# Pooled attention and a cosine MLP: weight differences in tiles of their own, two output buffers, and a first product copied by ScalarE

## The chip, the cores and the metric

The kernel runs on one core of one Trainium2 chip. The metric is device time in microseconds; the time before is the median of three runs. The profile is one execution of the program, with the span of its instructions in microseconds. In it PE is TensorE's matmuls and PEld its weight loads, DVE is VectorE, ACT is ScalarE, POOL is GpSimd and SP is SyncE; L402 is line 402 of the kernel.

## The reference

```
q, k, v: (8, 8, 576, 64) fp32                     # batch, heads, sequence, head size
k_p, v_p = mean of k, v over groups of 8 positions       # 72 pooled positions
attn = softmax(q @ k_p.T / sqrt(64)) @ v_p
x = attn with the heads side by side                     # 4608 tokens x 512
h = x @ w_in                                             # 512 x 2048
out = (h * cos(h)) @ w_out                               # 2048 x 512, fp32 out
```

## The kernel before

The 4608 tokens are nine tiles of 512, t = 0 to 8, and the eight batches of attention are woven into them: while tile t goes through the two layers, the attention of batch t + 1 is computed for the tiles to come. The schedule is written out by hand: each engine runs its instructions in the order in which the code gives them, and waits stand only where data or buffers ask for them.

A tile has two stages.

- The up stage, `up_mm` and `up_g`: 64 matmuls of 128x512 (L317) fill pairs of PSUM banks with h, two chunks of 128 hidden rows at a time. ScalarE makes cos of a bank as a Sin with a bias (L327), and VectorE multiplies bank and cosine into `g_sb` in bf16 (L331). The multiplication is what sets a bank free again. From tile 2 on, four pairs of banks go round, one of them the two `obanks`.
- The down stage. Tiles 0 and 1 use plain matmuls (`down_mm`, L334): four blocks of 128 tokens with 16 matmuls each, and a copy of each block by VectorE into an output buffer `o_two` (`down_out`, L339), from which SyncE's queue writes 64 rows at a time. Matmuls of attention stand between them; `fill` lists them with the number of down matmuls that stand ahead.

From tile 2 on (`FIRST = 2`) the down stage is a 2x2 block product with seven block products in place of eight (`down_products`). The tokens are halved (256 and 256), the hidden rows are halved (`HF` = 8 chunks of 128), the output columns are halved (`HM` = 256). Each product has 16 matmuls of 128x256 (L402) in one of two accumulators, A and Bb, each a PSUM bank; in the last tile each is two banks (`apart`), so that its halves can be read one by one. The products need sums of g, made by VectorE (`put_g12` L363 and L364, `put_g3` L368, `put_g4` L372, each in two halves: the first half in the up stage, the second in the down stage), and sums of w_out, which are made once. With b11, b12, b21, b22 the blocks of w_out:

```
w3 = b22 - b12     w2 = w3 + b11     w4 = b21 - w2     and     b12 - b11 for product 3
```

`put_weights` makes w3, w2 and w4 for the first half of the rows on GpSimd at the end of tile 0, and for the second half on VectorE between the up stage's g products of tile 1. The last difference, b12 - b11, is written in place over b12 (`put_first_weights`, L355). That can't be before the plain matmuls of tile 1 have read w_out, so the two instructions stand at the end of tile 1's down stage on VectorE, behind its last output copies and ahead of tile 2's first g product.

The order of the down stage from tile 2 on, from the code, with attention left out:

```
            product(0)
            product(1)
            put_g12(1)
            reads[0]()
            put_g3(1)
            reads[1]()
            put_g4(1)
            product(2)
```

`reads[0]` copies product 0 from A into `p1_sb` (L416); product 2 writes the same bank and so waits for this copy, and it also needs g2 from `put_g12`. `reads[1]` adds p1 to product 1 and writes the first output columns (L418); product 3 writes bank Bb and waits for it. In tiles 2 to 6 the scores of the next batch stand between products 0 and 1. In tile 7 only a small rest of them does, with its Exp on ScalarE, and in tile 8 nothing.

The output buffers of all tiles have one tag, `o_two`, of 128 x 2 x 512 fp32, which is 4 KB of each partition, and three of them go round. GpSimd adds up the groups of eight positions of k and v (`pool_add`, L151 to L159) in each tile up to tile 6, and issues the loads of the next batch.

Of the kernel before, what the change touches and what calls it, by code (L numbers as in the profile page):

```python
# [20 lines left out]
def kernel(  # L21
# [48 lines left out]
    HF, HT, HM = FFCH // 2, TILE // 2, d_model // 2  # L70
    g1, g2, g3, g4 = [wpool.tile([128, HF, HT], BF16, name=f"g{i}") for i in range(1, 5)]

    w2, w3, w4 = [[wpool.tile([128, 4, HM], BF16, name=f"w{k}{i}") for i in range(2)] for k in range(2, 5)]

    SpA = -(-Sp // 16) * 16
    kk = [wpool.tile([128, H, SpA], BF16, name=f"kk{i}") for i in range(2)]
# [258 lines left out]
                         rhs=w_out_sb[fc // 4][:, fc % 4, :], start=(fc == 0), stop=(fc == FFCH - 1))  # L335

    def down_out(t, ms, ps):
        o = msb.tile([128, 2, d_model], FP32, name="o_two", tag="o_two", bufs=3)[:, 0]
        nc.vector.tensor_copy(out=o, in_=ps)  # L339
        rows_of = out.rearrange("(b p t) m -> b t p m", b=B, t=ROW)  # L340
        for i, rows in enumerate(half):
            b_, pos = divmod((t * TILE + ms * 128) // 64 + i, ROW)
            nc.sync.dma_start(out=rows_of[b_, ORDER[pos]], in_=o[rows])

    def put_weights(i, eng, k=None):

        vec = eng.tensor_tensor
        (b11, b12), (b21, b22) = [(w[:, :, 0:HM], w[:, :, HM:]) for w in (w_out_sb[i], w_out_sb[i + 2])]
        for n, (w, x, y, op) in enumerate(((w3, b22, b12, SUB), (w2, w3[i], b11, ADD), (w4, b21, w2[i], SUB))):
            if k in (None, n):  # L350
                vec(out=w[i], in0=x, in1=y, op=op)

    def put_first_weights(i):
        w = w_out_sb[i]
        nc.vector.tensor_tensor(out=w[:, :, HM:], in0=w[:, :, HM:], in1=w[:, :, 0:HM], op=SUB)  # L355

    def g_part(f, t, f0, f1):
        return g_sb[:, f * HF + f0:f * HF + f1, t * HT:(t + 1) * HT]
# [15 lines left out]
    def down_products(t):  # L374

        def of(w, m=0):
            return lambda fc: w[fc // 4][:, fc % 4, m * HM:(m + 1) * HM]

        def part(x):
            return lambda fc, p: x[:, fc, p * 128:(p + 1) * 128]  # L380

        apart = t == NT - 1
        if apart:
            A, Bb = [[x[:, 0:HM] for x in two] for two in (obanks, (banks[1][:, 0, :], banks[2][:, 0, :]))]
        else:
            A, Bb = [[obanks[i][:, p * HM:(p + 1) * HM] for p in range(2)] for i in (1, 0)]
        products = [
            (A, True, part(g_part(0, 0, 0, HF)), of(w_out_sb[0:2])),
            (Bb, True, part(g_part(1, 0, 0, HF)), of(w_out_sb[2:4])),
            (A, True, part(g2), of(w2)),  # L390
            (Bb, True, part(g1), of(w_out_sb[0:2], 1)),
            (A, False, part(g3), of(w3)),
            (Bb, False, part(g4), of(w_out_sb[2:4], 1)),
            (A, False, part(g_part(1, 1, 0, HF)), of(w4)),
        ]
        mms = []
        for n, (bank, first, g, w) in enumerate(products):
            order = [(fc, p) for fc in range(HF) for p in range(2)]
            if apart and n == 6:
                order.sort(key=lambda x: x[1])  # L400
            for fc, p in order:
                mms.append(lambda bank=bank, first=first, g=g, w=w, fc=fc, p=p: nc.tensor.matmul(  # L402
                    bank[p], lhsT=g(fc, p), rhs=w(fc),
                    start=(first and fc == 0 and (apart or p == 0)), stop=(fc == HF - 1 and (apart or p == 1)),
                    skip_group_check=not first))

        p1, v16, q15 = [msb.tile([128, 2, HM], FP32, name=n, tag=n, bufs=1) for n in ("p1_sb", "v_sb", "q_sb")]
        o1, o2 = [msb.tile([128, 2, d_model], FP32, name="o_two", tag="o_two", bufs=3) for _ in range(2)]
        m1, m2 = slice(0, HM), slice(HM, d_model)

        def each(out, bank, other=None, m=slice(0, HM), tk=None):

            for p in range(2) if apart else (slice(0, 2),):
                ps = bank[p] if apart else obanks[1 if bank is A else 0].rearrange("p (a m) -> p a m", a=2)
                if other is None:
                    nc.vector.tensor_copy(out=out[:, p, m], in_=ps)  # L416
                else:
                    nc.vector.tensor_tensor(out=out[:, p, m], in0=ps, in1=other[:, p], op=ADD)  # L418
                if apart and tk is not None:
                    rows_out(t, tk, out, (p,), m, (nc.sync, nc.scalar))  # L420

        reads = [
            lambda: each(p1, A),
            lambda: each(o1, Bb, p1, m1, 0),
            lambda: each(v16, A, p1),
            lambda: each(q15, Bb, p1),
            lambda: each(o2, A, q15, m2, 1),
            lambda: (each(o1, Bb, v16, m2, 0), apart or rows_out(t, 0, o1)),
            lambda: (each(o2, A, p1, m1, 1), apart or rows_out(t, 1, o2)),
        ]  # L430
        return [mms[i * 2 * HF:(i + 1) * 2 * HF] for i in range(7)], reads
# [99 lines left out]
    for t in range(NT):  # L531
# [5 lines left out]
        for n, fp in enumerate(up_order(t)):  # L537
            up_mm(t, fp, 2 if n < 2 else 0)
            between = ()
            if t == 0:  # L540
                if fp == 4:
                    puts = pool_k_mm(1, obanks[0], 0, 2), pool_k_mm(1, obanks[1], 2, 4)
                elif fp in (5, 6):
                    g0 = 9 * (fp - 5)
                    puts = q_transpose_mm(1, obanks[0], g0, g0 + 5), q_transpose_mm(1, obanks[1], g0 + 5, g0 + 9)
                if fp in (4, 5, 6):
                    puts[0](vec)
                    between = ((puts[1], act),)
            up_g(t, fp, between)
            if t >= FIRST and 3 <= n < 6:  # L550
                (put_g12, put_g3, put_g4)[n - 3](0)
            if t == 1 and 3 <= n < 6:
                put_weights(1, nc.vector, n - 3)
            if 0 < t and b < B:
                if n == 0:
                    q_transpose(b)
                elif n == 2:
                    k_transpose(b)
# [36 lines left out]
        if t < FIRST:  # L595
            fi = 0
            for n, (ms, fc) in enumerate(mms):
                while fi < len(fill) and fill[fi][0] <= n:
                    fill[fi][1]()
                    fi += 1  # L600
                down_mm(obanks[ms % 2], ms, fc)
                if fc == FFCH - 1:
                    down_out(t, ms, obanks[ms % 2])
            if t + 1 == FIRST:
                for i in range(2):
                    put_first_weights(i)
        else:
            products, reads = down_products(t)

            def product(i, j=0, k=2 * HF):  # L610
                for mm in products[i][j:k]:
                    mm()

            us = BY_TOKENS
            later = []

            u0, u1, u2, u3 = [(b, us[i], banks[j]) for i, j in enumerate((2, 1, 0, 1))]
            ur = (t, REST, banks[2])

            def scores_of(*parts):  # L620
                for part in parts:
                    scores_mm(*part)
                for part in parts:
                    scores_exp(*part)

            def muls():
                while later:
                    later.pop(0)()

            steady, rest = b < B, t < B  # L630
            if rest:
                exp_tables()
            product(0)
            if steady:
                scores_of(u0, u1, u2)
            elif rest:
                scores_of(ur)
# [6 lines that stand above are left out]
            if steady:  # L644
                values(*u0, later)
            product(2)
            reads[2]()
            muls()
            if steady:
                values(*u1, later)  # L650
            product(3)
            reads[3]()
            muls()
            if steady:
                values(*u2, later)
            product(4)
            reads[4]()
            muls()
            if steady:
                scores_of(ur, u3)  # L660
            product(5, 0, 4)
            if rest:
                values(*ur, later)
            product(5, 4, 12)
            muls()
            if steady:
                values(*u3, later)
            product(5, 12)
            reads[5]()
            muls()  # L670
            product(6)
            reads[6]()
# [5 lines left out]
        if b + 1 < B:  # L678
# [1 line left out]
            load_q(b + 1)  # L680
            load_kv(b + 1, "v", v)
            if t == 0:
                put_weights(0, nc.gpsimd)
            pool_add(b + 1, "k")
            pool_add(b + 1, "v")
# [28 lines left out]
```

The softmax here doesn't subtract the row's maximum and nothing guards it: scores larger than these inputs give would overflow.

## Time and profile before

| | us |
|---|---|
| median of three runs (lowest, highest) | 294.95 (294.61, 295.21) |
| span of the profiled execution | 294.5 |
| VectorE: the two in-place differences, L355, start | 86.4 and 88.1 |
| the same, time of each | 1.76 and 1.82 |
| VectorE: copies of product 0, L416, full bank (six) | 0.68 |
| the same, half a bank (two, last tile) | 0.42 |
| TensorE's waits for that copy, in total (three) | 1.6 |
| output transfers, issue to landing: lowest, median, highest | 1.9, 2.4, 5.8 |

A row of a timeline gives start, duration, engine, line, operation, output <- inputs with their shapes, the number of instructions merged, and in brackets the idle time of the engine before it with what ended it. A row of busy times by stretch gives the stretch, its length, and then for each engine the busy time and the number of instructions. In the rows of groups the duration is the mean of one instruction in ns. Idle time of an engine that nobody waits for costs nothing. TensorE's granted clock is 0.999 in this run.

### The profile page before, as it was taken

What the parts mean: (1) busy time and instruction counts of PE and PEld (TensorE: products, weight loads), DVE (VectorE), ACT (ScalarE), POOL (GpSimd) and SP (SyncE); (2) the same over time, 40 slices, a digit from 0 to 9 for tenths busy, and PEclk for the clock granted to TensorE, in tenths of its full rate; (3) what the DMA queues carried; (4) which work ended last, traced back from release to release, by engine and by line L of the source; (5) the groups of instructions that cost most, each with busy time, mean ns of one, the idle gap of its engine ahead of it and who ended that gap; (6) DMA issues with size and microseconds to landing.
All of it is one profiled execution on the core that took longest, in us unless ns stands there. A gap on an engine that the chain in (4) does not pass through costs nothing. (4 is left out here: it accounts for less than half of the span.)

```text
span 294.5 us, 5317 instructions
## 1 busy us (share of the span) xinstructions
PE 282.1 (96%) x2096; PEld 174.0 (59%) x2120; DVE 226.6 (77%) x306; ACT 206.4 (70%) x261; POOL 148.4 (50%) x144
## 2 busy tenths in 40 slices
PE   8899999999999899999999999999999999999984
PEld 3545544444544587458745874588458844774673
DVE  5558547595489998799879887998798879846972
ACT  3786897469767688679967997699769976336500
POOL 8563079993995299536983599349900000000000
PEclk9999999999999999999999999999999999999999
DMA  7999999629817961969185929691840060005014
GB/s 163 205 207 206 207 205 204 139 52 148 168 37 137 139 104 26 200 89 163 19 182 89 169 45 195 92 174 28 173 73 2 4 142 0 2 21 122 2 36 107
DMA packets 44488, 32.95 MB, mean 112 GB/s; under 512 B 22192, under 2 KB 40112, under 8 KB 44464
## 3 DMA queue, kind: packets, MB, share of 16 engines
q0 software_dynamic: 19744, 18.07, 39.2%
q1 hardware_dynamic: 24080, 14.03, 22.2%
q10 hardware_dynamic: 640, 0.52, 0.7%
q8 instruction: 16, 0.26, 0.3%
q14 instruction: 8, 0.07, 0.1%
HBM read 36.70 MB, written 9.44 MB: 157 GB/s over the span
## 5 line engine op out<-in xcount | busy, mean ns | idle before, releaser
L317 PE MATMUL bank<-xT,w_in_sb 128*128 128x512 bf16 x503 | 114.7, 379 | 1.8 <-DVE g_sb L331 0.9
L327 ACT ACTIVATE cos<-bank,half_pi 128x1024 f32<-128x1024 f32 x65 | 71.4, 1113 | 48.5 <-PE bank L317 45.2
L317 PEld LDWEIGHTS <-w_in_sb 128*128 128x128 bf16 x576 | 56.0, 98 | 67.2 <-issue 1.5
L331 DVE TENSOR_TENSOR g_sb<-bank,cos 128x1024 bf16<-128x1024 f32 x65 | 78.4, 1220 | 22.1 <-ACT cos L327 22.0
L151 POOL TENSOR_TENSOR half_sums<-kv_st 72x512 f32<-72x512 bf16 x48 | 56.9, 1212 | 27.3 <-DMA kv_st<-in_k_dram 26.8
L262 DVE TENSOR_TENSOR xT<-bank,inv 64x512 bf16<-64x512 f32 (+1 forms) x72 | 45.3, 629 | 17.9 <-ACT inv L258 16.9
L257 ACT ACTIVATE inv<-bank 64x512 f32<-64x512 f32 (+1 forms) x72 | 39.1, 544 | 12.4 <-PE bank L251 11.2
L402 PEld LDWEIGHTS <-g 128*128 128x128 bf16 x448 | 42.9, 98 | 8.2 <-issue 3.3
L229 ACT ACTIVATE ex<-bank 72x1024 bf16<-72x1024 f32 (+1 forms) x40 | 35.1, 928 | 3.2 <-PE bank L222 3.0
L402 PEld LDWEIGHTS <-g_sb 128*128 128x128 bf16 x336 | 32.1, 98 | 6.9 <-issue 1.0
L153 POOL TENSOR_TENSOR half_sums<-half_sums 72x512 f32<-72x512 f32 x24 | 30.4, 1284 | 0.0
L334 PE MATMUL obank<-w_out_sb,g_sb 128*128 128x512 bf16 x123 | 29.9, 379 | 0.3 <-issue 0.2
L402 PE MATMUL obank<-w,g 128*128 128x256 bf16 x224 | 26.9, 272 | 1.7 <-DVE p_sb L416 1.6
L402 PE MATMUL obank<-w_out_sb,g_sb 128*128 128x256 bf16 x208 | 25.1, 273 | 0.3 <-DVE g_sb L331 0.3
L402 PE MATMUL obank<-w_out_sb,g 128*128 128x256 bf16 x192 | 24.8, 273 | 0.0
L258 ACT ACTIVATE inv<-inv 128x512 f32<-128x512 f32 (+1 forms) x36 | 21.0, 583 | 1.1
L251 PE MATMUL bank<-ex,vz 72*128 72x256 bf16 (+1 forms) x176 | 20.0, 243 | 0.0
L334 PEld LDWEIGHTS <-g_sb 128*128 128x128 bf16 x128 | 11.8, 97 | 12.5 <-issue 1.0
L251 PEld LDWEIGHTS <-vz 72*128 72x128 bf16 x176 | 13.7, 97 | 4.4 <-DVE xT L262 0.5
L156 POOL TENSOR_TENSOR kp<-half_sums 72x512 bf16<-72x512 f32 x12 | 15.0, 1270 | 0.5
L222 PE MATMUL bank<-qT,kk 64*72 64x256 bf16 (+1 forms) x192 | 13.2, 251 | 1.5 <-DVE g_sb L331 0.6
L402 PE MATMUL obank<-w,g_sb 128*128 128x256 bf16 x112 | 13.4, 273 | 0.0
(83 smaller groups left out, 253.6 us busy)
## 6 DMA issues: line engine op xcount, KB each, us to landing
out_dram<-o_two SPq DMA_DIRECT2D x64, 128.0 KB, 2.4
kv_st<-in_v_dram POOLq DMA_DIRECT2D x8, 576.0 KB, 13.6
kv_st<-in_k_dram POOLq DMA_DIRECT2D x7, 576.0 KB, 7.8
q_b<-in_q_dram POOLq DMA_DIRECT2D x6, 576.0 KB, 9.9
w_in_sb<-in_moe_w_in_dram POOLq DMA_DIRECT2D x4, 512.0 KB, 13.1
w_out_sb<-in_moe_w_out_dram POOLq DMA_DIRECT2D x4, 512.0 KB, 18.5
q_b<-in_q_dram POOLq DMA_DIRECT2D x4, 288.0 KB, 11.7
g_sb<-in_k_dram SPq DMA_DIRECT2D x1, 576.0 KB, 3.7
```

The lines of the kernel that those rows point to most:

```text
L151: add(out=s[:, h:h + 2], in0=x[:, h:h + 2, 0:4, :], in1=x[:, h:h + 2, 4:8, :], op=ADD)
L153: add(out=s[:, h:h + 4, 0:2, :], in0=s[:, h:h + 4, 0:2, :], in1=s[:, h:h + 4, 2:4, :], op=ADD)
L229: nc.scalar.activation(out=ex[:, 0:nh * n].rearrange("p (a n) -> p a n", a=2), in_=pair[:Sp, :, 0:nh * n // 2], func=ACTF.Exp, scale=scale ...
L251: nc.tensor.matmul(pair[:, hp, (i // 2) * n:(i // 2 + 1) * n], lhsT=vz[b % 2][:, pj, 2 * hp:2 * hp + 2, :].rearrange("p a d -> p (a d)"), ...
L257: nc.scalar.activation(out=inv[half[1 - hp]], in_=pair[half[1 - hp], hp, 0:w], func=ACTF.Ln)
L258: nc.scalar.activation(out=inv, in_=inv, func=ACTF.Exp, scale=-1.0)
L262: nc.vector.tensor_mul(out=x_out(b, u, half[hp]), in0=cols(pair[half[hp], hp, :], u), in1=cols(inv[half[1 - hp]], u))
L317: nc.tensor.matmul(h[j] if h is obanks else h[:, j, :], lhsT=w_in_sb[fc // 4][:, ki, (fc % 4) * 128:(fc % 4 + 1) * 128], rhs=xT[:, ki, t * ...
L327: nc.scalar.activation(out=c, in_=ps, func=ACTF.Sin, bias=half_pi[:, :1])
L331: nc.vector.tensor_mul(out=o, in0=ps, in1=c)
L334: nc.tensor.matmul(o, lhsT=g_sb[:, fc, ms * 128:(ms + 1) * 128], rhs=w_out_sb[fc // 4][:, fc % 4, :], start=(fc == 0), stop=(fc == FFCH - 1))
L402: mms.append(lambda bank=bank, first=first, g=g, w=w, fc=fc, p=p: nc.tensor.matmul(bank[p], lhsT=g(fc, p), rhs=w(fc), start=(first and fc ...
```

## The change

The differences b12 - b11 get tiles of their own, w1, so that w_out stays as loaded. With that they no longer have to stand behind tile 1's matmuls: they are made on VectorE in tile 1's down stage, one behind its third down matmul and one behind its fifth, in the order of the code. The two tiles take 4 KB of each partition, and one of the three output buffers is given up for them. The third edit moves the copy of product 0 to ScalarE in tiles 7 and 8 (`t >= B - 1`), where VectorE makes the second half of g1 and g2 just ahead of it; the aim is that the bank comes free while VectorE is still at these sums.

```
-    w2, w3, w4 = [[wpool.tile([128, 4, HM], BF16, ...) for i in range(2)] for k in range(2, 5)]
+    w1, w2, w3, w4 = [[wpool.tile([128, 4, HM], BF16, ...) for i in range(2)] for k in range(1, 5)]
...
-        o = msb.tile([128, 2, d_model], FP32, name="o_two", tag="o_two", bufs=3)[:, 0]
+        o = msb.tile([128, 2, d_model], FP32, name="o_two", tag="o_two", bufs=2)[:, 0]
...
-    def put_first_weights(i):
-        w = w_out_sb[i]
-        nc.vector.tensor_tensor(out=w[:, :, HM:], in0=w[:, :, HM:], in1=w[:, :, 0:HM], op=SUB)
+        for k in ks:
+            out, x, y, op = {1: (w1, b12, b11, SUB), 3: (w3, b22, b12, SUB), 2: (w2, w3[i], b11, ADD),
+                             4: (w4, b21, w2[i], SUB)}[k]
+            eng.tensor_tensor(out=out[i], in0=x, in1=y, op=op)
...
-            (Bb, True, part(g1), of(w_out_sb[0:2], 1)),
+            (Bb, True, part(g1), of(w1)),
...
-        o1, o2 = [msb.tile([128, 2, d_model], FP32, name="o_two", tag="o_two", bufs=3) for _ in range(2)]
+        o1, o2 = [msb.tile([128, 2, d_model], FP32, name="o_two", tag="o_two", bufs=2) for _ in range(2)]
...
-                    nc.vector.tensor_copy(out=out[:, p, m], in_=ps)
+                    (nc.scalar.copy if t >= B - 1 else nc.vector.tensor_copy)(out=out[:, p, m], in_=ps)
...
-            if t + 1 == FIRST:
-                for i in range(2):
-                    put_first_weights(i)
+                if t == 1 and n in (2, 4):
+                    put_weights(n // 2 - 1, nc.vector, (1,))
```

The other sums of weights keep their place, their engine and their order.

More of the change, by code (lines that the diff above doesn't have):

```diff
@@ L71 @@
     g1, g2, g3, g4 = [wpool.tile([128, HF, HT], BF16, name=f"g{i}") for i in range(1, 5)]
-    w2, w3, w4 = [[wpool.tile([128, 4, HM], BF16, name=f"w{k}{i}") for i in range(2)] for k in range(2, 5)]
+    w1, w2, w3, w4 = [[wpool.tile([128, 4, HM], BF16, name=f"w{k}{i}") for i in range(2)] for k in range(1, 5)]
     SpA = -(-Sp // 16) * 16
@@ L343, in down_out, with put_weights @@
             nc.sync.dma_start(out=rows_of[b_, ORDER[pos]], in_=o[rows])
-    def put_weights(i, eng, k=None):
-        vec = eng.tensor_tensor
+    def put_weights(i, eng, ks=(1, 3, 2, 4)):
         (b11, b12), (b21, b22) = [(w[:, :, 0:HM], w[:, :, HM:]) for w in (w_out_sb[i], w_out_sb[i + 2])]
-        for n, (w, x, y, op) in enumerate(((w3, b22, b12, SUB), (w2, w3[i], b11, ADD), (w4, b21, w2[i], SUB))):
-            if k in (None, n):
-                vec(out=w[i], in0=x, in1=y, op=op)
-    def put_first_weights(i):
-        w = w_out_sb[i]
-        nc.vector.tensor_tensor(out=w[:, :, HM:], in0=w[:, :, HM:], in1=w[:, :, 0:HM], op=SUB)
+        for k in ks:
+            out, x, y, op = {1: (w1, b12, b11, SUB), 3: (w3, b22, b12, SUB), 2: (w2, w3[i], b11, ADD),
+                             4: (w4, b21, w2[i], SUB)}[k]
+            eng.tensor_tensor(out=out[i], in0=x, in1=y, op=op)
     def g_part(f, t, f0, f1):
@@ L549 @@
             up_g(t, fp, between)
-            if t >= FIRST and 3 <= n < 6:
+            if t == 1 and 3 <= n < 6:
+                put_weights(1, nc.vector, ((3, 2, 4)[n - 3],))
+            if t > 1 and 3 <= n < 6:
                 (put_g12, put_g3, put_g4)[n - 3](0)
-            if t == 1 and 3 <= n < 6:
-                put_weights(1, nc.vector, n - 3)
             if 0 < t and b < B:
@@ L682 @@
             if t == 0:
-                put_weights(0, nc.gpsimd)
+                put_weights(0, nc.gpsimd, (3, 2, 4))
             pool_add(b + 1, "k")
```

## The prediction

> **What bounds the kernel now.** I read the page's busy times first, then busy times cut by tile, then the chain and the waits of TensorE, then the timelines of the tiles that stand out.
>
> ```profile
> PE 282.1 (96%) x2096; PEld 174.0 (59%) x2120; DVE 226.6 (77%) x306; ACT 206.4 (70%) x261; POOL 148.4 (50%) x144
> ```
>
> TensorE is busy 282.1 of 294.5 us, so only what shortens its gaps shortens the kernel. The busy times by stretch, one tile each (tiles 2, 3, 7 and 8, from the first up matmul to the next tile's first), show where the gaps are:
>
> ```profile
> 84.12:116.02 31.90, 30.23 (x223) 19.63 (x224) 30.52 (x37) 23.93 (x31) 23.05 (x21) 1.00 0.58 97
> 116.02:145.95 29.93, 29.67 (x224) 19.68 (x224) 25.93 (x34) 24.10 (x32) 19.18 (x18) 1.00 0.70 121
> ...
> 235.74:263.20 27.46, 26.70 (x193) 17.55 (x193) 21.44 (x28) 14.82 (x17) 0.00 (x0) 1.00 0.17 39
> 263.20:290.57 27.37, 26.42 (x176) 17.11 (x175) 19.95 (x31) 8.96 (x9) 0.00 (x0) 1.00 0.27 60
> ```
>
> The columns are length, then busy time of PE, PEld, DVE, ACT, POOL. Tiles 3 to 6 take 29.93 us each (starts 116.02, 145.95, 175.88, 205.81, 235.74) with one PE wait of 0.16 us. Tile 2 runs the same instructions and takes 1.97 us longer; its DVE is busy 30.52 of 31.90 us. Its timeline tells why:
>
> ```profile
> 86.39 3.49 DVE L355 TENSOR_TENSOR w_out_sb<-w_out_sb 128x1024 bf16<-128x1024 bf16 x2
> ...
> 89.81 3.67 DVE L331 TENSOR_TENSOR g_sb<-bank,cos 128x1024 bf16<-128x1024 f32 x3
> ...
> 97.32 1.89 PE L317 MATMUL bank<-xT,w_in_sb 128*128 128x512 bf16 x8 [0.93 <-DVE g_sb L331]
> ```
>
> The two in-place weight differences stand on DVE ahead of the tile's first g product. That starts at 89.81, 5.7 us after the tile's start; in tile 3 it is 119.96-116.02 = 3.9. TensorE then waits 0.93 us for a bank.
>
> In tiles 7 and 8 the wait is another one, the copy of the first product out of its bank:
>
> ```profile
> 252.88 0.69 DVE L364 TENSOR_TENSOR g<-g,g_sb 128x1024 bf16<-128x1024 bf16 x1
> 253.49 0.68 DVE L416 COPY p_sb<-obank 128x512 f32<-128x512 f32 x1
> 254.23 1.91 PE L402 MATMUL obank<-w,g 128*128 128x256 bf16 x16 [0.66 <-DVE p_sb L416]
> ...
> 280.34 0.69 DVE L364 TENSOR_TENSOR g<-g,g_sb 128x1024 bf16<-128x1024 bf16 x1
> 280.95 0.75 DVE L416 COPY p_sb<-obank 128x256 f32<-128x256 f32 x2
> 281.42 2.13 PE L402 MATMUL obank<-w,g 128*128 128x256 bf16 x16 [0.75 <-DVE p_sb L416]
> 283.39 1.91 PE L402 MATMUL bank<-w_out_sb,g 128*128 128x256 bf16 x16
> ```
>
> These tiles have no or few attention matmuls between products 0 and 1, so DVE has not caught up with the last g product and the second half of g1 and g2 when product 2 wants the bank. The chain that ended last begins at exactly this copy:
>
> ```profile
> 281.37 0.34 DVE p_sb L416
> ```
>
> **What the Trainium skill says.** "SBUF — State Buffer", section "Who interferes with whom": a DVE instruction with two SBUF inputs contends with a GpSimd instruction that reads SBUF. The trace agrees: the 128x1024 bf16 sum takes 0.68 us with POOL idle, but 1.25 at 61.95 and 1.76 and 1.82 at L355, each beside a POOL sum. "ScalarE: Activation LUTs", section "What ACT_TABLE_LOAD costs": an ACTIVATE with immediate operands takes 186 ns + 0.833 ns per element, an estimate of 0.61 us for 512 columns; the trace's nearest row, the ScalarE copy of 128x512 bf16 out of a bank (L204), takes 0.58. "Perfetto Trace Analysis", section "Optimizing Scalar/DVE Operations", advises moving work to ScalarE where DVE is saturated; in tiles 7 and 8 ScalarE is busy 14.82 and 8.96 us.
>
> **The change part by part.**
>
> *Weight differences.* The two sums leave the start of tile 2 and stand in tile 1's down matmul, behind the last g product (67.72 to 68.94) and ahead of the first output copy. DVE is idle there until 71.44 (2.50 us, waiting for PE), and POOL is idle from 67.4 to 72.37, so each should take the free 0.68: 1.4 us, inside the idle 2.5. Even at 1.8 each they end at 72.5, and what is queued behind them is one output copy, 1.1 us late, whose bank TensorE wants only a chunk of 16 matmuls later. Cost nothing; operands and the loads they wait for have long landed.
>
> In tile 2, DVE's first g product can start when its cos is done (87.15+1.1 = 88.2). Of the 1.97 us, 0.25 stays: the first 23 up matmuls take 5.59 instead of 5.34 because they wait for the last attention product into xT, which isn't touched. The up stage then ends at 98.19 instead of 99.05: 0.86. The product stage took 116.02-99.05 = 16.97 against 145.95-129.84 = 16.11 in tile 3, another 0.86. I take that too as DVE's lateness: the waits there are 0.27 for g_sb and 0.19 for p_sb, and late DVE sums met POOL's pooling sums, which a DMA landing starts at 102.22 (L364 took 1.53). On tile 3's schedule L363 and L364 stand at 100.8 to 102.2, just ahead of it; L368 and L372 meet POOL as L372 does in tile 3, without a PE wait. So 1.72 us; 0.86 is the low end.
>
> *First product on ScalarE, tile 7.* Products follow at 1.75 us (255.97, 257.72, 259.47), so product 2 could start at 251.65+1.75 = 253.40; it starts at 254.23, a loss of 0.83. On ScalarE the copy is queued behind the exponential of the rest segment (252.18, 0.59), so starts at 252.8 and takes 0.58 (L204) to 0.70 (the half-bank Sin, 1.40 for two); I take 0.61. It ends at 253.4 and the matmul starts near 253.46. The second half of g2 is done at 253.57 and wanted eight matmuls later, at 254.3. Saved 0.77 (range 0.65 to 0.83). Behind the copy on ScalarE stand the logarithms of the rest segment, 7.57 us idle before: nothing. No table load is added: Sin and Exp already alternate with plain copies at 8.26 to 32.13 without one.
>
> *Tile 8.* Product 2 could start at 278.76+1.75 = 280.51. The second copy releases its second matmul, so its real start is 283.39-1.75 = 281.64: a loss of 1.13. ScalarE is free at 277.21+1.11 = 278.32; product 0 ends near 278.9; two copies of 0.42 (DVE's time for the shape) end at 279.8, before 280.51. The second half of g2 ends at 281.03, wanted at 280.51+8x0.109 = 281.38. DVE, without the copies, runs g3 at 280.95 to 281.63 and the two reads of bank B to about 282.3; product 3's second matmul wants it at 282.37. That is close, so I allow 0.1 to 0.3. The later reads had 0.99 us idle each. Saved 1.1 (range 0.8 to 1.13).
>
> *Two output buffers.* This frees what the two sums occupy and adds waits. In tiles 2 to 8 a buffer is written again about 20 us after its four transfers are issued, which land in 1.9 to 3.5. In tile 0 the third and fourth copies (51.86, 52.72) now wait for transfers issued from 44.58 to 46.45, landing in 5.0 to 5.7, so by 50.3 and 52.2: about half a microsecond to spare. Should it be missed, queued behind on DVE is tile 1's first g product, with 3.04 us idle before it. Cost nothing.
>
> Product 3 only reads another tile. Sum: 1.72 + 0.77 + 1.1 = 3.6; 294.95 - 3.6 = 291.35, so 291.4.
>
> **Rivals.**
> - *Tile 2 gets half*: POOL's start is set by a DMA, not by DVE, and with it the slow sums remain; product stage keeps its 0.86, and the copies give 0.65 and 0.8. Gain 0.86+0.65+0.8 = 2.3: 292.6. For it: 0.03 us between L364 and POOL's start. Against: tile 3 overlaps them too, unharmed.
> - *The copies give nothing*: the wait moves from the copy to g2 or bank B's reads. Gain 1.7: 293.2. For it: DVE is the busy engine there. Against: g2's second half is done 0.3 us or more before its matmul.
> - *Slower*: two buffers make DVE wait for landings, which hold a bank. One microsecond in each of seven product tiles gives 294.95+7-3.6 = 298.4. Against: 20 us of distance to landings of 3.5 at most.
>
> **How the numbers follow.** Chances: forecast 0.73, half 0.18, copies nothing 0.06, slower 0.03. The top of the gain is 1.72+0.83+1.13 = 3.7, with the 0.3 us spread of the runs: 290.9 or a little under. At the other end the half case at 292.6 is taken in, with little beyond. Range 290.8 to 292.8. Faster 0.96, same 0.01, slower 0.03.
>
> **What would show it.** Right: tile 2 takes about 30.2 us with no PE wait for g_sb in its up stage; the w sums take about 0.7 us near 69; in tiles 7 and 8 PE waits for p_sb are gone or under 0.1, tile lengths 26.7 and 26.3; the idle before DVE's output writes names no out_dram transfer. Wrong: a PE wait for g or o_two in place of p_sb, sums above 1.2 us in tile 1, or tile 2 still over 31.

## The result and the profile after

The changed kernel takes 294.02 us (median of four runs, 293.49 to 294.39) beside 294.93 us for the kernel before (four runs, one more than in the table above): ratio 0.9968, interval 0.9946 to 0.999, 0.3 to 1.6 us faster. The forecast was 291.4 with a range of 290.8 to 292.8. Compared once more in the runs below, both on one chip, the same two kernels gave 293.47 and 295.67: ratio 0.993, interval 0.9917 to 0.9942, 1.7 to 2.5 us faster. The two intervals don't meet, and why is open. Both are far from the forecast gain of 3.6.

The profile after, the busy times of the page:

```profile
PE 283.2 (97%) x2120; PEld 174.1 (59%) x2120; DVE 223.8 (76%) x303; ACT 208.0 (71%) x264; POOL 147.1 (50%) x144
```

Busy times by stretch of the changed kernel, for tiles 2, 3, 4, 7 and 8, in the same columns as before (length, then PE, PEld, DVE, ACT, POOL):

```profile
85.12:115.69 30.57, 30.06 (x226) 19.66 (x224) 27.08 (x35) 23.98 (x31) 21.09 (x20) 1.00 0.62 101
115.69:145.99 30.30, 29.88 (x227) 19.77 (x224) 26.80 (x34) 24.41 (x32) 21.14 (x20) 1.00 0.68 119
145.99:175.92 29.93, 29.77 (x226) 19.71 (x224) 25.58 (x34) 24.12 (x32) 19.19 (x19) 1.00 0.70 121
235.79:262.43 26.64, 26.64 (x195) 17.58 (x193) 20.83 (x27) 15.30 (x18) 0.00 (x0) 1.00 0.18 40
262.43:288.66 26.23, 26.20 (x178) 17.07 (x175) 19.28 (x29) 9.61 (x11) 0.00 (x0) 1.00 0.28 63
```

Tile 7 is 27.46-26.64 = 0.82 us shorter and tile 8 27.37-26.23 = 1.14, nearly what was forecast. TensorE has no gap left in them. Tile 2 is 31.90-30.57 = 1.33 shorter in this pair of profiles, and tile 3 is 0.37 longer. But tile 2 starts at 85.12 instead of 84.12, and of this 1.0 us, 0.90 was lost before tile 1 started (53.42 instead of 52.52), ahead of the moved differences. How tiles 7 and 8 run now is seen in the timeline of the changed kernel:

```profile
252.23 0.59 ACT L229 ACTIVATE ex<-bank 72x512 bf16<-72x512 f32 x1
252.72 0.57 ACT L412 COPY p_sb<-obank 128x512 f32<-128x512 f32 x1
252.93 0.69 DVE L360 TENSOR_TENSOR g<-g,g_sb 128x1024 bf16<-128x1024 bf16 x1
253.45 2.78 PE L398 MATMUL obank<-w,g 128*128 128x256 bf16 x24
...
278.08 0.65 ACT L412 COPY p_sb<-obank 128x256 f32<-128x256 f32 x2 [0.52 <-PE obank L398]
...
279.57 0.69 DVE L360 TENSOR_TENSOR g<-g,g_sb 128x1024 bf16<-128x1024 bf16 x1
279.73 1.91 PE L398 MATMUL obank<-w,g 128*128 128x256 bf16 x16
```

In tile 7 the copy now runs beside the second half of g2 (L360); in tile 8 both copies are done before it. In both tiles product 2 starts 1.75 us behind product 1 with no wait in brackets. The chain that ended last, which began at the copy, is now products alone over its last pieces:

```profile
279.90 1.75 PE obank L398 x16
281.64 1.75 PE bank L398 x16
```

The weight differences cost nothing where they are now, as was forecast: 0.68 us each, done at 71.14, and the output copy behind them still waits for TensorE (VectorE's timeline of the changed kernel):

```profile
67.59 2.34 DVE L331 TENSOR_TENSOR g_sb<-bank,cos 128x1024 bf16<-128x1024 f32 x2
69.86 1.28 DVE L351 TENSOR_TENSOR w<-w_out_sb 128x1024 bf16<-128x1024 bf16 x2
72.44 0.69 DVE L339 COPY o_two<-obank 128x512 f32<-128x512 f32 x1 [1.30 <-PE obank L334]
```

So two of the three terms hold, and the missing gain has to do with tile 2 and with what the profile of before is worth there. One more number points the same way: the execution in that profile took 296.27 us, 1.3 above the median of the kernel before.

### The profile page after: what moved, and what is told of

It reads as the page before. It is cut to its first block, busy times and chain, and to the rows that moved or that the text cites. A ratio compares the mean times of both kernels' runs of the same rounds, so it can differ in the third digit from the quotient of the medians.

```text
span 292.6 us, 5344 instructions
## 1 busy us (share of the span) xinstructions
PE 283.2 (97%) x2120; PEld 174.1 (59%) x2120; DVE 223.8 (76%) x303; ACT 208.0 (71%) x264; POOL 147.1 (50%) x144
## 4 chain that ended last, share of the span: by engine, by line
PE 48%; DVE 2%; ACT 1%; issue 0%
PE bank L317 21%; PE obank L398 19%; PE obank L317 3%; PE bank L251 2%; PE bank L398 2%; DVE g_sb L331 1%; ACT cos L327 1%; PE bank L222 1%; DVE xT L262 0%; DVE o_two L414 0%
## 5 line engine op out<-in xcount | busy, mean ns | idle before, releaser
L151 POOL TENSOR_TENSOR half_sums<-kv_st 72x512 f32<-72x512 bf16 x48 | 56.3, 1200 | 26.6 <-DMA kv_st<-in_k_dram 26.2
L398 PE MATMUL obank<-w,g 128*128 128x256 bf16 x320 | 37.9, 272 | 0.0
L334 PE MATMUL obank<-w_out_sb,g_sb 128*128 128x512 bf16 x128 | 30.8, 379 | 0.6 <-DMA w_out_sb<-in_moe_w_out_dram 0.6
L153 POOL TENSOR_TENSOR half_sums<-half_sums 72x512 f32<-72x512 f32 x24 | 29.9, 1266 | 0.0
L334 PEld LDWEIGHTS <-g_sb 128*128 128x128 bf16 x128 | 11.9, 98 | 13.1 <-issue 1.6
L398 PE MATMUL obank<-w_out_sb,g 128*128 128x256 bf16 x96 | 13.3, 273 | 0.0
```

The source lines that it names most:

```text
L151: add(out=s[:, h:h + 2], in0=x[:, h:h + 2, 0:4, :], in1=x[:, h:h + 2, 4:8, :], op=ADD)
L153: add(out=s[:, h:h + 4, 0:2, :], in0=s[:, h:h + 4, 0:2, :], in1=s[:, h:h + 4, 2:4, :], op=ADD)
L334: nc.tensor.matmul(o, lhsT=g_sb[:, fc, ms * 128:(ms + 1) * 128], rhs=w_out_sb[fc // 4][:, fc % 4, :], start=(fc == 0), stop=(fc == FFCH - 1))
```

## Experiments

### The parts one by one

The kernel before once more, the copies alone, the weight differences with two buffers alone, and the whole, on one chip.

```
act_only, against the kernel before:
-                    nc.vector.tensor_copy(out=out[:, p, m], in_=ps)
+                    (nc.scalar.copy if t >= B - 1 else nc.vector.tensor_copy)(out=out[:, p, m], in_=ps)
w1_only, against the changed kernel:
-                    (nc.scalar.copy if t >= B - 1 else nc.vector.tensor_copy)(out=out[:, p, m], in_=ps)
+                    nc.vector.tensor_copy(out=out[:, p, m], in_=ps)
```

> The kernel before, unchanged. Its profile on record has a span of 294.5 us and belongs to an execution of 296.27 us, 1.3 above its median of 294.93; the changed kernel's executions all stand 1.78 above their spans, so the median execution of before should have a span near 293.15. Theory 1 (tile 2's loss is the same in each execution, and the profile of before was slow in some other stage, as the loads at the start): tile 2 takes 31.9 us again and another stage is about 1.3 us shorter. Rival 2 (the loss in tile 2 varies with the time at which the pooling's load lands): tile 2 takes nearer 30.5 us. Time within 0.3 of 294.9.

> Only the copies of product 0 in tiles 7 and 8 move to ScalarE; in-place weight differences and three buffers as before. The comparison of the two profiles gives 0.9 us less in tile 7 and 1.1 in tile 8. Theory 1 (these are gains in every execution): 293.0 us, 0.9935 of before. Rival 2 (they are given back at the end, in output transfers): under 0.5 us less, over 294.4.

> The weight differences in their own tiles, made in tile 1, and two output buffers; product 0 is copied by VectorE throughout. Theory 1 (tile 2 gains 1.0 to 1.5 us net, and the wait of 0.9 us for the load of w_out in tile 0 that the changed kernel's profile shows is a chance of that execution): 293.7 us, faster by 1.0 to 1.5. Rival 2 (that wait comes with this part, in each execution): 294.6 to 295.0, about no change. Rival 3 (this part costs more than it gives): 295.9, since the whole gained 0.9 and the copies 1.9.

> The changed kernel, unchanged, beside the others on one chip. 294.0 us, 0.997 of before. Theory 1 (chance at the start): in its profile the wait for the load of w_out in tile 0 may be absent, and the span then near 291.7. Rival 2 (comes with the change): a wait of 0.5 to 0.9 us there again.

| kernel | median us | ratio to before (295.67) and interval | tile 7, tile 8 |
|---|---|---|---|
| before_again | 295.65 | 1.0002 (0.9986 to 1.0017) | 27.5, 27.4 |
| act_only | 293.96 | 0.9948 (0.9929 to 0.9967) | 26.6, 26.2 |
| w1_only | 295.55 | 1.0001 (0.9988 to 1.0014) | 27.5, 27.4 |
| after_again | 293.47 | 0.993 (0.9917 to 0.9942) | 26.6, 26.2 |

The copies on ScalarE give 1.0 to 2.1 us by the interval, 1.96 in the profiles, and aren't given back at the end. The weight differences with two buffers give nothing, within 0.4 us either way, where 1.0 to 1.5 were expected. And the kernel before, profiled again, has no loss in tile 2's up stage. This is its timeline, the rows of VectorE and POOL around the start of tile 2 (first up matmul at 84.36):

```profile
83.72 4.94 POOL L151 TENSOR_TENSOR half_sums<-kv_st 72x512 f32<-72x512 bf16 x4
86.64 2.57 DVE L355 TENSOR_TENSOR w_out_sb<-w_out_sb 128x1024 bf16<-128x1024 bf16 x2
88.62 2.94 POOL L153 TENSOR_TENSOR half_sums<-half_sums 72x512 f32<-72x512 f32 x2
89.13 3.68 DVE L331 TENSOR_TENSOR g_sb<-bank,cos 128x1024 bf16<-128x1024 f32 x3
```

The two in-place differences take 2.57 us here, not 3.49, the first g product starts 4.77 us into the tile, not 5.69, and the up stage takes 14.07 us, not 14.93. The whole tile takes 30.37 us, not 31.90. Theory 1 had tile 2's loss in each execution and is refuted; rival 2 holds in that the loss varies. What it varies with is looked at further below.

The 1.0 us ahead of tile 2 in the changed kernel's profile isn't the change either. TensorE waits 0.5 to 0.6 us for a load of w_out in tile 0's down stage (L334) there, but also in before_again and act_only, which have tile 0's copies as before. It isn't in after_again or in the first profile of before, and tile 0 takes 35.6 us in both of them, against 36.3 where the wait is.

### What the differences cost at most, the slack, and what makes them slow

```
no_first, against the kernel before:
-            if t + 1 == FIRST:
-                for i in range(2):
-                    put_first_weights(i)
first_twice:
+                for _ in range(2):                    # around the loop over i
pool_off:
-            pool_add(b + 1, "v")
+            if b + 1 != 3:
+                pool_add(b + 1, "v")
two_buffers:
-    ... tag="o_two", bufs=3)                          # both places
+    ... tag="o_two", bufs=2)
```

> The kernel before without the two in-place weight differences at all, so product 3 multiplies by b12 in place of b12 - b11; everything else as before. The upper bound of what moving them can give. Theory 1 (the loss in tile 2 is there only where both of them meet POOL's sums late; in most executions they end in time): 295.2 us or no change within 0.3, up and down stage of tile 2 14.07 and 16.3 us. Rival 2 (they cost 1.7 us in each execution, as the profile on record shows): 293.9 us.

> The kernel before with the two in-place differences made twice over, four instructions in place of two, so product 3 multiplies by b12 - 2 b11. Measures DVE's slack at the start of tile 2. Theory 1 (slack of about 1 us: pairs of 2.4 to 2.6 us end in time, one of 3.6 costs 0.9 in the up stage): four take 4 to 6 us, the up stage of tile 2 is 15.5 to 17 us in place of 14.07, time 297 to 298. Rival 2 (there is no slack, each us on DVE costs one): 3 to 4 us longer, over 298.2.

> The kernel before without POOL's sums of v for batch 3, the ones that run beside the in-place differences, so batch 3 uses old values; the loads stay. Theory 1 (what makes the differences slow is POOL's sums[...]): each difference takes 0.68 us in place of 1.0 to 1.8, the first g product of tile 2 starts 3.9 to 4.2 us after the tile, and the time is within 0.3 of before, as most executions don't lose anything there. Rival 2 (in-place operands or strided columns make them slow): 1.3 to 1.8 us each again.

> The kernel before with two output buffers in place of three, nothing else. All theories: no change within 0.3 us, and no wait of DVE for an output transfer. If two buffers cost something that the moved differences give back, it is 0.5 us or more here. Its profile is also one more sample of the in-place differences beside POOL: pair of 2.4 to 3.6 us, and only a pair over 3 us goes with an up stage of tile 2 over 14.1.

| kernel | median us (before 295.53) | ratio and interval | in-place differences, us | first g product after the tile's start | up stage of tile 2 |
|---|---|---|---|---|---|
| no_first | 295.37 | 1.0 (0.9985 to 1.0014) | none | 4.19 | 14.07 |
| first_twice | 300.09 | 1.0151 (1.0132 to 1.017) | 0.80, 1.76, 1.75, 1.75 | 8.03 | 17.27 |
| pool_off | 295.7 | 1.0008 (0.9998 to 1.0017) | 0.68, 0.68 | 4.19 | 14.07 |
| two_buffers | 295.56 | 1.0002 (0.999 to 1.0014) | 0.68, 1.76 | 4.57 | 14.07 |

(The up stage is from its first weight load to the first of the products, and the product stage from there to the next tile's first. The prediction counted the product stage by matmuls, which makes it 0.1 us shorter.) Leaving the differences out altogether gains nothing that can be measured, so moving them can't either: at most 0.45 us on the average of executions. With POOL's sums of v away each difference takes 0.68 us, so POOL is what makes them slow, not in-place operands. Two buffers cost nothing, and no wait of VectorE names an output transfer.

With the differences made twice the loss is in the up stage, 17.27-14.07 = 3.20, and 1.05 more in the product stage (17.27 against 16.22). From this run and from the first profile of before comes the slack: 8.03-3.20 = 4.83 and 5.69-0.86 = 4.83. The first g product may start 4.83 us after the tile, 0.64 later than its cosine allows, before TensorE loses anything; past that each microsecond costs one. The expected time of 297 to 298 was too low by two, as I had let only part of the delay through and none of the product stage's. By its time alone this run falls on the side of rival 2, which had no slack at all; against that rival stand the start times, with 0.64 us of slack, and the kernel before, which pays nothing measurable for its two differences.

### What decides whether the loss is there

Four profiles with a single in-place pair now had it beside POOL's sums, and the loss was in one, the first profile of before. There POOL's sum at L153 starts at 86.38 and VectorE's difference at 86.39, and both differences are slow:

```profile
86.38 2.96 POOL L153 TENSOR_TENSOR half_sums<-half_sums 72x512 f32<-72x512 f32 x2
```

In two_buffers the order is the other way round:

```profile
87.61 2.36 DVE L355 TENSOR_TENSOR w_out_sb<-w_out_sb 128x1024 bf16<-128x1024 bf16 x2
87.64 3.47 POOL L153 TENSOR_TENSOR half_sums<-half_sums 72x512 f32<-72x512 f32 x2
89.90 3.68 DVE L331 TENSOR_TENSOR g_sb<-bank,cos 128x1024 bf16<-128x1024 f32 x3
```

VectorE is 0.03 us ahead, its first difference takes 0.68 and only the second 1.76, and now it is POOL that is held up: 3.47 for two sums that take 2.5 alone. A theory from this: who comes first holds the other up, and TensorE loses only if POOL is first. To test it, VectorE has to be made late by something that doesn't itself hold up POOL. The first two tries used a memset, the third a copy out of a PSUM bank; each also ran in the changed kernel as a control, at the end of tile 1's down stage.

```
nudge, nudge_longer, nudge_bank, against the kernel before, each one of the lines:
             if t + 1 == FIRST:
+                nc.vector.memset(warm[:, 0:256], 0.0)
+                nc.vector.memset(g4.rearrange("p f n -> p (f n)")[:, 0:768], 0.0)
+                nc.vector.tensor_copy(out=warm[:, 0:256], in_=obanks[1][:, 0:256])
                 for i in range(2):
                     put_first_weights(i)
```

> The kernel before with one memset of 128x256 bf16 (about 0.25 us on VectorE, into a tile not in use at that time) ahead of the two in-place differences. In four profiles of kernels with the in-place pair, the pair cost TensorE time in one, where POOL's sum at L153 started 0.01 us ahead of the first difference; where VectorE was ahead by 0.02 to 0.1 us, or met POOL otherwise, none. Theory 1 (the order of arrival[...] decides): POOL now arrives first in nearly each execution, both differences take over 1.6 us, the up stage of tile 2 is 14.8 to 15.3 us in place of 14.07, and the time is 1.0 to 2.0 us over before. Rival 2 (the loss on record had another cause; a small delay is lost in slack): up stage 14.07, time within 0.3 of before.

> The changed kernel with the same memset at the same place, the end of tile 1's down stage on VectorE. Theory 1: [...]no change: 293.5 to 294.0 us, up stage of tile 2 14.07. Rival 2 (the delay itself costs): as much more as in the other run.

The small memset delayed VectorE by 0.14 us only, and VectorE was still 0.14 us ahead of POOL: differences of 0.72 and 1.75, up stage 14.06, 295.8 us beside 295.48 (1.0011, 0.9997 to 1.0024). Inconclusive. The control took 294.17 us (0.9944, 0.9924 to 0.9964), as the changed kernel.

> As the run with the small memset, but 768 columns in place of 256: the first memset delayed VectorE by only 0.14 us and VectorE still started 0.13 us ahead of POOL's sum. This one should delay it by 0.3 to 0.4 us, past the range in which POOL's sum started in the profiles (2.48 to 2.77 us after the up stage of tile 2). Theory 1 (the order of arrival[...] decides): both differences take over 1.6 us, the first g product of tile 2 starts 5.8 to 6.3 us after the up stage, which takes 14.8 to 15.3 us in place of 14.07; time 1.0 to 2.0 us over before. Rival 2 (the order of arrival is not what decides): the pair keeps 2.4 to 2.6 us, up stage under 14.2, time within 0.5.

> The changed kernel with the same memset of 768 columns at the end of tile 1's down stage on VectorE. Theory 1: no change against the changed kernel, 293.3 to 294.2 us, up stage of tile 2 14.07, since the delay is inside the 0.65 us of slack[...]. Rival 2 (the delay costs by itself): as much more as in the other run.

By its times this run falls on the side of rival 2. Its timeline:

```profile
87.75 0.38 DVE L605 MEMSET g<- 128x384 uint32 x1
87.78 3.69 POOL L153 TENSOR_TENSOR half_sums<-half_sums 72x512 f32<-72x512 f32 x2
88.04 2.30 DVE L355 TENSOR_TENSOR w_out_sb<-w_out_sb 128x1024 bf16<-128x1024 bf16 x2
```

POOL's first sum started 0.26 us ahead of the difference and yet was the one held up, 2.02 us in place of 1.28, while the difference took 0.63. The theory of the order doesn't explain this. The memset in front, 0.03 us ahead of POOL, can't have done it alone. In the control the same memset was 0.02 us ahead of the same sum, with no difference behind it, and POOL's two sums took their free 2.5:

```profile
87.88 0.38 DVE L603 MEMSET g<- 128x384 uint32 x1
...
87.90 2.51 POOL L153 TENSOR_TENSOR half_sums<-half_sums 72x512 f32<-72x512 f32 x2
```

The run with the difference behind the memset took 295.88 us beside 295.74 (1.0014, 1.0 to 1.0028). The first g product starts 4.91 us after the tile, and the up stage takes 14.14: the slack of 4.83 again, to 0.01. The control's time was 293.76 us (0.9933, 0.9911 to 0.9954).

> The kernel before with one copy of 128x256 from a PSUM bank (about 0.33 us on VectorE, into columns that are written over later) ahead of the two in-place differences. Theory 1 (the order of arrival[...] decides): POOL's sum at L153 starts 2.5 to 2.8 us after the up stage of tile 2 and is first, not slowed (1.28 us); both differences take over 1.5 us; the first g product starts at 5.8 to 6.3; the up stage is 14.8 to 15.3 us in place of 14.07, the time 1.0 to 1.8 us over before. Rival 2 (the order is not the cause): the pair stays at 2.4 to 2.6 us, up stage under 14.2, time within 0.5 of before.

> The changed kernel with the same copy at the end of tile 1's down stage on VectorE. Theory 1: 293.3 to 294.2 us as without it, up stage of tile 2 14.07: 0.33 us lies inside the slack of 0.65. Rival 2 (the delay costs by itself): as much more as in the other run.

With the copy from a bank in front, POOL is first. The rows of VectorE and POOL, then of TensorE where it waits (tile 2 starts at 84.13):

```profile
86.41 0.41 DVE L605 CAST g<-obank 128x256 bf16<-128x256 f32 x1
86.65 2.95 POOL L153 TENSOR_TENSOR half_sums<-half_sums 72x512 f32<-72x512 f32 x2
86.74 3.41 DVE L355 TENSOR_TENSOR w_out_sb<-w_out_sb 128x1024 bf16<-128x1024 bf16 x2
89.68 1.60 POOL L159 TENSOR_TENSOR vz<-half_sums 72x512 bf16<-72x512 f32 x1
90.08 3.67 DVE L331 TENSOR_TENSOR g_sb<-bank,cos 128x1024 bf16<-128x1024 f32 x3
...
97.59 1.89 PE L317 MATMUL bank<-xT,w_in_sb 128*128 128x512 bf16 x8 [0.91 <-DVE g_sb L331]
```

It is the picture of the first profile of before, row by row. The differences take 1.73 and 1.76 us, POOL's first sum its free 1.27; the up stage takes 15.18 us and the product stage 17.08. The median goes to 297.09 us beside 295.64, and the comparison gives 1.0042 (1.0027 to 1.0057). An instruction that delays VectorE by 0.33 us costs 0.8 to 1.7 us. In the changed kernel it costs nothing: 293.48 us, 0.9925 (0.9907 to 0.9942), up stage 14.06.

The delay by itself isn't what costs. With the memset of 768 columns the first difference started even later, 2.68 us after the tile against 2.61 here; there POOL was the one held up, and the up stage took 14.14 us, not 15.18. So the loss comes when POOL's sum holds up the pair, and in this test that was brought about by letting POOL arrive first.

The 16 profiles of this case together show how far the order of arrival goes as a rule. In 34 places a 128x1024 bf16 sum of VectorE and one of POOL's sums of k or v start within 0.3 us of each other. In 20 of them VectorE is first or level: its sum takes 0.68 to 0.80 us, and POOL's 1.41 to 1.79, where 1.14 to 1.28 is free. In 14 POOL is first, and in 13 of these its sum is free and VectorE's takes 1.40 to 1.82. The one exception is the difference behind the longer memset.

They also show how often POOL is first at the start of tile 2, and why. VectorE's pair, with nothing put ahead of it, starts 2.27 to 2.29 us after the tile in six profiles. POOL's first sum at L153 is in 15 profiles: it starts at 2.26 in the first profile of before, at 2.30 to 2.56 in 13 others and at 4.26 in before_again. So POOL would have been ahead of the undelayed pair in one of 15. POOL starts its sums of k when the load of k has landed, and from there on it runs almost without a gap. Its wait for that load was between 4.98 and 5.25 us, shortest in the first profile of before; in the 14 profiles other than before_again the start of L153 follows this wait to within 0.05 us. That it is the load which sets the lead is read from the traces and wasn't tested by a run.

## Why the prediction was wrong

- **What bounds the kernel**: right. The gain came from TensorE's gaps, and nothing else.
- **Tile 7**: forecast 0.77, measured 0.82. The copy took 0.57 us, below the 0.61 taken. The reason given for no table load was misread: one does stand in the stretch named, at 17.82, between exponentials and sines, though none at a copy. ScalarE's count rises by three instructions, the three copies, so no load was added.
- **Tile 8**: forecast 1.1, measured 1.14. The two copies took 0.37 each, and bank B was read in time.
- **Weight differences in tile 1, and two buffers**: forecast at no cost, measured at none (w1_only, two_buffers).
- **Tile 2**: the step that failed: "Of the 1.97 us, 0.25 stays", and from that "So 1.72 us; 0.86 is the low end". The subtraction is nearly sound for that one execution: its up stage loses 0.86, which is gone in the changed kernel's profile, and its product stage another 0.86, of which 0.46 is gone (16.97 to 16.51 by matmuls). But the prediction took a loss from one execution as the loss of each. For a single pair it is there only when POOL's sum comes ahead of VectorE's difference; in three of four profiles of kernels with the in-place pair it wasn't, and without the differences the median doesn't move. The term should have been near 0, with a top of 1.7, and the low end of 0.86 was no low end. With it at 0 the sum is 0.77+1.1 = 1.9 and the forecast 293.1. The later comparisons of the changed kernel and its three controls lie at 0.9925 to 0.9944, or 1.7 to 2.2 us; the one on record, at 0.9, is short even of that.
- **"Against: tile 3 overlaps them too, unharmed"**: not quite. In the changed kernel's profile POOL's sums meet g3 in tile 2 (L364, 1.66 us), the product into xT comes late, and TensorE waits 0.28 us at the scores behind it. That tile's product stage takes 16.61 us and tile 3's 16.59, in place of 16.22. In tile 3 that is so in this profile alone, but tile 2's product stage takes 16.36 to 16.61 us in all six profiles of kernels with the moved differences. The rival "tile 2 gets half" had this kind of loss in part right, though not where the missing gain lay.

What the prediction set down as showing it right came or nearly came (tile 2 took 30.57 us for about 30.2), and nothing of what would show it wrong. All of it looked at the changed kernel alone, and the missing gain lay in what the kernel before loses.

Two warnings stood in the material. The profiled execution took 1.3 us longer than the median of the timed ones, close to what tile 2 lost. And the two rows behind the loss, POOL at 86.38 and VectorE at 86.39, are 0.01 us apart, and neither row shows a wait for the other: such a wait can't be counted on. That the profile on record was the one of 15 with POOL ahead was bad luck; to sum it without a chance was not. The prediction named the collision with POOL, as the reason for the slow sums, and gave it to the wrong question: whether it would stay after the change, not whether it was there in each execution before.

What stays open: why the load of k lands earlier or later from one execution to the next, why the difference behind the longer memset wasn't held up, and why the comparison on record came out below the later ones. The start of tile 1 lies between 52.5 and 53.7 us in the 16 profiles, with waits for loads in some and not in others; with four runs a median may move by some tenths from that alone, but that this made the difference isn't shown.

## What to carry to other kernels

Before a gap in one profile is counted as gain, compare that execution's time with the median of the timed runs, and look at the start times of the rows that make the gap: where two engines that don't wait for each other arrive within tens of nanoseconds, the gap is a matter of chance and belongs in the forecast with its chance. Waits that follow from one engine's own order, as the copy behind g1 and g2 here, repeat to a few hundredths of a microsecond and can be summed as they stand: tile 7 took 27.46 us in all ten profiles with the copy on VectorE and 26.63 or 26.64 in all six with it on ScalarE. A delayed instruction costs only past its slack, which two profiles with different delays give by subtraction, 4.83 us here from three runs.

## What was not expected of the hardware

- A lead of 0.01 us (first profile of before) or 0.09 us (nudge_bank) of POOL's sum over VectorE's, against a lag of 0.03 us (two_buffers), decided about 1 us on VectorE, and with the slack used up about 1.5 us of kernel time: the pair took 2.3 to 2.6 us with VectorE first or POOL met midway, 3.4 to 3.5 with POOL first.
- The engine that started first was not always the one that went through: behind a memset of 128x768 bf16, carried out as 128x384 uint32, VectorE's difference took 0.63 us and POOL's sum 2.02, though POOL had started 0.26 us ahead of the difference (nudge_longer, one profile). The memset without the difference behind it didn't hold POOL up.
- ScalarE's copy of 128x512 fp32 from a bank took 0.57 us against VectorE's 0.68, and of 128x256 0.37 against 0.42.
